# A new hand-kept instruction order, a recalibrated planner and a shorter last block in a fused attention and gated-MLP kernel

## The chip, the cores and the metric

The kernel runs on one core of a Trainium2 chip. The metric is the device time of one execution in microseconds, the median of several runs. Profiles come from one profiled execution, whose own time is given beside its span. TensorE is called PE here (its weight loads PEld), VectorE DVE, ScalarE ACT, GpSimd POOL, and the queue that issues the transfers SP.

## The reference

Two branches work on the same x (2048 rows of 512) and are mixed by a gate of one number per row:

```python
x = A_x                                    # (1, 2048, 512)
g = sigmoid((x * gate_w).sum(-1, keepdims=True))
# A: 32 query heads of 16, one shared key head and value head (wk, wv: 512 x 16)
q = heads(x @ wq); k = x @ wk; v = x @ wv
p = softmax(einsum("bhqd,bkd->bhqk", q, k) / 4)
a = heads_back(einsum("bhqk,bkd->bhqd", p, v)) @ wo
# B: a gated MLP with 1792 hidden columns
b = (sigmoid(x @ w_gate) * (x @ w_up)) @ w_down
return g * a + (1 - g) * b
```

All is fp32. A value may be split into a rounded part and a rest (`fp32r`), so that one product becomes three matrix multiplications.

## The kernel before

**The work.** Rows are cut into four blocks of 512 (`NB`). Attention goes in 32 units (`NU`), each a block of query rows with four heads. A unit has three kinds of PE work. First come 64 *maxima*: a matmul of 62 rows by 512 columns (line 1040), whose largest value per row DVE takes (line 1042). Then come 64 *scores*: a matmul of 64 rows by 512 columns (line 1049), of which ACT takes the exponential into a tile `p` (line 1051). Last come 16 *values* steps (line 931): each multiplies four `p` tiles with V, four 128x32 column tiles side by side, into bank 7. The MLP and the output projection are cut into 4404 *fill* matmuls of 64 rows by 512 columns (line 1019), which belong to jobs: `g` and `u` for gate and up, `d` for down, `a` and `e` for the output projection.

Maxima, scores and fills use half of the array's rows each, so they come in pairs: one matmul on the upper half, one on the lower, at the same time. Values use the whole array in four column tiles.

**The order.** Nothing is scheduled at run time. `ORDER` is a string, found by a search beforehand and kept in the file, of one character per step:

- a hex digit is a step of two halves: its two base-4 digits say what the upper and the lower half do (0 nothing, 1 a maximum, 2 a score, 3 a fill), so `f` is two fills and `6` a maximum beside a score;
- `V` is one values step, `T` turns the maxima of a finished unit (line 916), `G` is one group of the first projections (lines 798 and 855), and `.` is a pause of 25 units of the planner's clock that gives no instruction.

`plan()` walks through the string with a `State`, a model of the engines with a clock in units (one step of two halves is 100), and writes down the actions in the order in which they are then recorded for each engine. Each engine runs its own list in order; a last loop of `tile_kernel` ties them together so that no scheduler moves anything. So the constants at the top of the file do two things: they decided which orders the search held to be possible, and they set where the planner puts the work of DVE, ACT, POOL and SP between the steps.

**What the planner reckons with.** Steps share seven PSUM banks (0 to 6). `issue_m` takes the bank that has been free longest and marks it busy until `LATE` (from the step to the reader's start), plus the reader's cost on its engine's own clock (`RED` for a maximum), plus `TAIL` and `FREE`. `issue_s` does the same with `EXP`, `issue_f` and `settle` with the readers of a finished fill job, `issue_t` and `issue_g` likewise. A values step may come when all four of its exponentials are seen (`can_v`). `IN`, `OUT` and `FIRST` are what a change between paired steps and values costs on the planner's clock, `VALUES` a values step itself.

**The last block.** When the string is done, the last unit's sums (bank 7) are copied out in two halves on ACT, turned on PE, divided on DVE by their own sums, turned back, copied (three on ACT, one on DVE) and multiplied with the last rows of `wo` into banks 3 to 6. For two of the four output tiles PE first puts the sum so far into the bank (`so_far`, line 1077); ACT then copies those two out (line 1106) and DVE adds the other two (line 1108). Each tile is stored by its own transfer (line 1109).

Of the kernel before, what the change touches and what calls it, by code (L numbers as in the profile page):

```python
# [18 lines left out]
P = 128  # L19
# [20 lines left out]
LATE, FREE = 230, 50  # L40

RED, EXP, COPY, MIX, TAIL = 260, 212, 230, 275, 40


IN, OUT, FIRST, VALUES, TURN = 45, 45, 57, 371, 75
# [56 lines left out]
class State:  # L102
# [157 lines left out]
    def event(self, what, args):  # L260
# [15 lines left out]
        elif what == "send_max":  # L276
            self.max_ready[args[0]] = self.send(4, 16)
        elif what == "store":
            self.after(self.send(5, 136) + SAFE, "sums", *args)
        elif what == "sums":  # L280
            self.after(self.send(1, 8) + 2 * SAFE, "invert", *args)
        elif what == "invert":
            self.after(self.on("dve", self.now, 120), "send_inverse", *args)
        elif what == "send_inverse":
            self.after(self.send(1, 8) + SAFE, "spread", *args)
        elif what == "spread":
            u = args[0]
            at = self.send(1, 128)
            if u % 2 or u == NU - 2:
                self.task(2, at + 2 * SAFE, "divide", u)  # L290
        elif what == "out":
            at = self.send(1, 256)
            self.ba_release(args, at)
# [85 lines left out]
    def settle(self):  # L379
        for h in range(2):  # L380
            while self.at[h] is not None and self.at[h] == self.jobs[self.job[h]].n:
# [4 lines left out]
                if j.kind == "g":  # L386
                    self.acts.append(("gate", h, j, i))
                    at = self.on("act", at, COPY)
                elif j.kind == "u":
                    slot, free = self.take_h()  # L390
                    self.acts.append(("gated", h, j, i))
                    at = self.on("dve", max(at, free), MIX)
# [3 lines left out]
                self.free[i] = at + TAIL + FREE  # L396
# [8 lines left out]
    def gather(self, j, h, i, second, at):  # L405

        key = (j.b, j.i % NT)
        if key not in self.parts:
# [3 lines left out]
            return self.on("act", at, COPY)  # L412
        self.parts[key] += 1
        if not second and j.kind != "e":
# [3 lines left out]
            return self.on("act", max(at, free), COPY + 30)  # L418
        self.acts.append(("part", h, j, i, "sum"))
        at = self.on("dve", at, MIX)  # L420
# [38 lines left out]
    def issue_m(self, h):  # L459
# [4 lines left out]
        if self.mp[h] == min(self.mp) and self.mp[h] % (2 * NC) == 0:  # L464
            u = self.mp[h] // (2 * NC) - 1
            self.acts.append(("max_finish", u))
            self.maxima.append((u, self.on("dve", 0, 170)))

    def issue_s(self, h):
# [5 lines left out]
        at = self.on("act", self.now + LATE, EXP)  # L475
        self.free[i] = at + TAIL + FREE
# [3 lines left out]
        self.exps[e][1] = max(self.exps[e][1], at + TAIL + 80)  # L480
# [5 lines left out]
    def issue_v(self):  # L486
# [7 lines left out]
        if c == NC - 1 and u < NU - 1:  # L494
            self.acts.append(("finish", u))
            at = self.on("act", self.now + LATE, COPY) + TAIL
# [6 lines left out]
    def issue_t(self):  # L503
# [4 lines left out]
        at = self.on("dve", self.now + LATE, 260)  # L508
# [14 lines left out]
    def issue_g(self):  # L523
# [9 lines left out]
        else:  # L533
# [5 lines left out]
            if what == "keys":  # L539
                self.ba_take(("v", b), 1)  # L540
                at = self.on("dve", self.on("act", at, 250) + 50, MIX)
# [8 lines left out]
        self.free[i] = at + TAIL + FREE  # L550
# [24 lines left out]
    def step(self, code):  # L575
# [10 lines left out]
        elif code in "VG":  # L586
            if not self.full:
                self.now += IN
            if code == "V" and self.last != "V":
                self.now += FIRST  # L590
# [16 lines left out]
    "GGGGGGGG554G551G554GG551G541G554G55GG517G5d7ffG55fffd7ffGd7ffdf7ffdf7ffdff7cGd75ffG55fffd7ffGT5fffdf5ff7fG9ff7df"  # L607
    "fefffb7fff97fedfe7f9ff6fdbf7efdb7fedf6f35V969V696V9694V969V696V965Vb9ff7f9fe7ff9f6V97efdf6fedfb7f9ff7edef7f9VV69"
    "6V95eVTbff7dfe7f9ff7efdb7fedf6ff9ff6fdbf7bd.V696V9616V969Vb7efdf7fdbe7ffdbf6d.V696V969V55bVebf6ff9f7fedb7fedf9V6"
    "69VV69fbff6fd7bf9V6f9fff6deVT69V6f9f7fbdef7f9fe7fdbc6V969V696Vd56Vbbdeff6fdbbf6ff9f7d7VVd6bdff7fedbeff6fdbbV696V"  # L610
    "969V6bdeff6fbdbf7d7deVV6b9fff6fdbef6ff9f7bef9ff6.V55bVV9e6fffdb7ebfdefTfbf6ff97f9VVV697fff9fe7fedfaV696V969V6dbf"
    "7f9fe7ff9f6ffde7bVV9e7fefdf7bdfe7f9f7dVV6db7ffedbef7bf9f7eef5..V969V69eV696V97f9ff6ff9f7eff9ff6V9T6Vb96V9e7eff9f"
    "e7bf9fe7efd7VV969V6df6ff9ff6fdbf7bfde7VV9e7bff9f7eef9ff6fdbef6ff9f7d7VV96ffdff7bdebV696V969V69aV6dbf7f9fe7fedf6V"
    "V96bfff9f7edf6ff9fbef7dff6bVVT96V969.V6bdfef6fdbbf6ff9f7ebf9ff5VVV69feff6fbdef6fbdbVV69feff6fdb7f9ff6fbdf7ef9f7f"
    "d7edV5b7ffefd7V969V69a4V9652VV96fbff9f7edfe7f9ff6VV9fe7bf9feef7bedfb7fed7.VV9T6V96ffdf6fd7V9fbfef7bd7eV9f6fbfd7e"
    "dbV69ffefb7edbV696V969Vf5ebfef7bf9fe7ef9fe7VV969V6fdbf7edfb7fedf6fdb7VV9eb7ff9fe7ef9fe7bfde3V696V95b7V9a7VTeefdf"
    "f6bdbff6fdbd.VV6b7eff9f7ebf9ff7d7deVV6bedff6fbdbf6fbdef7df5V696VV9bf6ffdfb7ef9f7def6VV96bfff9fe7bf9fe7efdbf6V96d"
    "8VV697V96fdff6ff9f7dV6bdfef6fdbfb6ff9fef6fdbf75V97dV6T9V696V97efdf6fbdff6f9VV6bdbff6fdbef6ff9f7bef9ff6fV969V69aV"
    "7f9fe7efd7f9f7dVVV69feff6fbdbf6fbdef7bfedb7eVV965V96Vb9ef7fed7f9V69efff7db7eVT5bVe9fe7fbdef6fbdbff5faVV697fff9fe"
    "7fdef5ffbe7V969V696V979Vf6fedfb7ef9fe7df6f17VV96ffdf6fbdfb7f9V69efff6fdb7f9ff6fbdf7ef9fe.V69aV659V69VVTbef7ff9ef"  # L620
    "6ff9fb7ef9fe7df7df6VVV96bfff9f7edf6V96fbff9f7edf6ff9VV69bfff6ff9ef6ff9fb7ef9fe7dVV69ff7fdfb7ebff9f7edVV696V9eb7V"
    "9e7eff9f7ebfdef6fdbV696V9694V969V7VTedbfff6bedff6fbdbf6V97deff6ff9f7bfdef7bdV696V965VV96bfff9f7edf6ff9f7eVV96fbf"
    "fdfe7bf9fe7ef9fe7VV965Vbedbff6fdbef6ff9f7dbVV69ff7f9fe7ff9f6ffde7V969V696VT58Vebdef7bf9fe7ef9f7df278VV9e7eff9fe7"
    "bf9fe7efdb36V596VV9e7ffdb7edf7df6VV96ffbfdfb7ef9fe7bf9fe7fde7VV969Ve7bf9fe7ef9fe7bf9ff6fedff57d7VVV9fe7bf9fe7ef5"
    ".V9692VT689V6dbf7f9fe7ff9f6ffde7dVV6bbdff6fbf9fe7ef5ffaVV9692V5b79Ve6bffdef6fdbbf7ef9f7ebf9ff5V69f7ffdf7edeV6a9V"
    "696V596VV9b6fff9fe7bfd7edbVV6b9fff6fedbf7edfb7edf7dfTVVV69fbff6fd78c9Ve7fefdb6fbV9e7eff9fe7bV96feff9f7d7VV97efef"
    "9fe7bf9fe7efdb36Vd69fff7fbde7ff9V697V97fdeV69eV6bbdff6fbdef6fbdf7dbV696V969VV6Tbfffd7e9V6b9fff6fde7f9V696.V979V6"
    "edfbf5febf7efbd7d7VV9e6fff9f7ebf9ff6fdebf5.V696Vdfb7f9ff6dfe7f9VV6bedff7bdebf7ef9fe7bf9f7dVV69eV696V9e6fff9f7bef"
    "5VVTbedfff6bdbff6fd7df6VV9b6fff9f7dV6bedff6fbdbf6fbdef7bf9fe7df6fd7VVV96bfff5febeV96aVdb7efdbf7ef9f7ebf9ff6fdef7"
    "5VVV97efbf9f7edfe7.V969V6b9fff6fdebf6ff9f7deV696V96bV969VT56..Vbefdbf6fdbef6ff9f7d7VV96bfff9fe7ef9fe7bfde36V969V"  # L630
    "6d6dVV69ffbf7fbdbf6fbdef6VV96bfff9fe7bf9f7edVV6fbdef6fbdbf6fbdef7df6fbdVVV6bf9ff6fbdef6fd7dVV6Tbfffd7bbdf7fedbef"
    "f6fdbV696V969V696V96fdff6fbdf7bf9ff7edbf7f9V69f7V96dV6f5effbfd7e8eV969V69ff7f9fe7ff9f6ffde7V969V696VV9f6fdf6fbdf"
    "f6f9ff7bd2VVTb7efff9e7bff9f7edf6c.V9694VV9e6fff9f7ebf9ff6fde73aVV969V6bdeff6fdbbf6ff9f7ebf9ff5VV7ef9f7efde7fbde7"
    "V969VV697fff9fe7fdef6ffdb78VV9e6fff9f7ebf9ff6fde739V69V696VbT9V69ff7f9fe7ff9f6ffde..6VV969V6df6ff9ff6fdbf7bfde7V"
    "V9e6fff9f7bef9ff6fdbef6ff9f7d7VV96dfff7fbdebV696VV9e6fff9f7bef9ff6fd7dVV6bbdff6fbdef6fbdbf7ef5V969V696V9T6V969V6"
    "bfdef7bdebf7ef9f7ebf9ff5VVV69efff6fbdef6fbdbVV69feff6fdb7f9ff6fbdf7ef9f7fd7edV6bdfff7dbV6961V6b9V696VV9e6fff9fb7"
    "efdb7d7VV9e6fff9feb7f9fef7ef9f7deVV6T94V9fe7fdbf6fV96fbff9f7deV6deeffb7bdbV6fbdef6fbd7VV9fe7bf9fe7ef9fe7dV697ff."
    "V969V6db7ff9fe7fdef6ffdb78V969V696V969V69ff7f9fe7ff9f6ffde72VV9T7V9fef6f9fef6fbdbf6ff9VV6fbdef6fbdbf6fbdef7bf9f7"
    "d7VVV9e6fff9f7eef9ff6.V969V7edbf7efd7d7bVV97efef9fe7bf9fe7efdbf7ebdef7V969VV696V9f6fbf9f7efde7fbde7fd7f9VVVT6bff"
    "ff9ef6ff9fe7V969V6f97ff9V69efff6fdb7f9ff6fedf7bf9f7fed7dff6VVV9eb7ff9fe7ef9fe7bfdef6fd7dV69ff7ffdb7bfdf6VV9692V6"  # L640
    "9bfff6fdb7f9ffe7efdV696V96aV969V6a9V6T9V6dbf7f9fe7ff9f6ffd7d4VVV97efbf9fe7ef9fe7bfdeV696V96bVb597Vf9e7ffdfe7edff"
    "6f9V69bV6edfbf6fdbf7bfedb7efd7bf9VVV6ebdff6fbdef5fb7eVV9eb7ff9fe7ef9fe7dVVTbe7fff9e7bff9f7fede7fbd41V696V969V696"
    "V96bfff9f7edf6ff9VV6fbdef6fbdbf6fd7df7bVe9fe7fV969V6fbdef7d7d7VV9ef6ff9fb7ef9fef6ff9fb7ef9f7d7V96dV696VVTbfedff6"
    "fbdbf6fd7bf9V696V96eV95efffb7f9f7efdef7d7VV97bfdfefe7bdefb7dfeb24VV9e7bff9f7eef9ff6fdbe35V69.6....8V595V69VV69fe"
    "ff6fd7bV9a7fff9fe7eV96bfff9fe7ef9f7fedf6VVT96Vbbefdf7bef9ff6fdf6f9VV696Vb9ff7f9V697fffeed7fdbfaV6dbfeff6fbdbf6fb"
    "d7fed7dVV7b9ff7efde7befd7faV969V696Vbde7bfde7f9f7dVVV69efff6fd7bf9ff7edbfef7db7eVVT96Vb9ef7fedbf6fbdef6ff9f7d7f9"
    "VVV6bf9ff6fedbf6fbdV696V9a6V5fbdef7fbde7ff9fe7fdbf6fdfb7eV95f7fffed7V9a6V969V569VV6b9fff6fed7fbde7V96dV69fbff7f9"
    "f6ffde7bfdfe7beVV9T6V9f6fbf9f7deV69ffefb7edbV696Vb9e7ffedbf6V9e6fff9f7d7VV96fbffdfe7dfb7edff639VV6dbfbf6fbf9f6fe"
    "f9ffe4VV969V6bedff6fdbbf6fff97edVV69bV69efffbefbfefbfefbVVaTaVa.fefbfeVbeb2VVbfebffffeffbfefffbebeVVbebffefVaeVb"
    "bffebfefbfVea8Va..2Va8.2Va.8....2Va8..2Va8....2Va8..2.V.a8..2VaeceVaececc8Vaecc8c8V88.....VV"  # L650
# [11 lines left out]
def tile_kernel(ctx, tc, x_in, wq, wkv, wo, wg, wu, wd, consts_in, out):  # L662
# [405 lines left out]

# [4 lines left out]
    for i in range(2):  # L1073
# [88 lines left out]
```

## Time and profile before

| what | value |
|---|---|
| median of 3 runs | 1652.71 us (1652.61 to 1653.44) |
| profiled execution, its own time | 1652.89 us |
| its span in the trace | 1651.0 us |
| granted PE clock | 1.0 |
| busy share of the span: PE, PEld, DVE, ACT, POOL | 100%, 58%, 86%, 73%, 47% |
| mean DMA traffic | 60 GB/s |

1.9 us of the profiled execution's time lie outside the span. Busy time of PE is modelled from the instructions' sizes and overlaps, so 100% says only that PE always had something under way; the distance between the starts of its instructions is what can be read. The chain of work that ended last goes back from the last instruction through whatever released each one.

### The profile page before, as it was taken

The page shows a single profiled execution, that of the slowest core. Times are in us where ns is not written, and L with a number is a line of the kernel's source. Part 1 is how long each engine was busy: PE and PEld are TensorE (multiplying, and loading weights), DVE is VectorE, ACT ScalarE, POOL GpSimd, SP SyncE. Part 2 cuts the span into 40 slices and gives each one's busy share as a digit, 9 for nine tenths or more (in the row PEclk, how much of TensorE's full clock was granted, in tenths as well). Part 3 has the DMA queues.
Part 4 walks back from the last instruction along what each step waited for, and adds up shares of the span by engine and source line. Part 5 has one row for each costly group of instructions (what it writes and reads, how often), then busy time and mean ns, then how long its engine had stood idle before and what let it go on. Part 6 is the DMA issues. An engine that isn't in the chain of part 4 may idle for free.

```text
span 1651.0 us, 33584 instructions
## 1 busy us (share of the span) xinstructions
PE 1643.5 (100%) x12958; PEld 965.2 (58%) x12958; DVE 1424.5 (86%) x2419; ACT 1207.4 (73%) x2277; POOL 773.3 (47%) x598
## 2 busy tenths in 40 slices
PE   9999999999999999999999999999999999999998
PEld 7765556565555565656555656655566555555553
DVE  5799989899899998999988898989989989988941
ACT  4267777778767777687777777777777777777787
POOL 4524433548443336536455435444835432753341
PEclk9999999999999999999999999999999999999999
DMA  7412001115111112104111111211511101210001
GB/s 236 145 49 69 28 25 61 31 56 145 41 31 57 56 37 75 44 29 117 56 57 43 44 52 50 64 29 57 145 31 41 58 28 44 94 43 31 8 31 43
DMA packets 52085, 98.31 MB, mean 60 GB/s; under 512 B 17944, under 2 KB 19096, under 8 KB 50900
## 3 DMA queue, kind: packets, MB, share of 16 engines
q1 hardware_dynamic: 51924, 96.16, 19.0%
q8 instruction: 102, 1.67, 0.4%
q14 instruction: 59, 0.48, 0.1%
HBM read 74.25 MB, written 8.90 MB: 50 GB/s over the span
## 4 chain that ended last, share of the span: by engine, by line
PE 98%; ACT 1%; DMA 1%; SPq 0%; DVE 0%; issue 0%; ACTq 0%; DVEq 0%
PE bank L1019 31%; PE bank L931 30%; PE bank L1040 18%; PE bank L1049 17%; PE bank L798 2%; DMA consts<-consts 0%; PE bank L916 0%; SPq L895 0%; ACT x L717 0%; DVE qs L903 0%; DMA stage<-qd 0%; PE bank L1101 0%; SPq L702 0%; DVE ks L848 0%; ACT q L877 0%
## 5 line engine op out<-in xcount | busy, mean ns | idle before, releaser
L1042 DVE TENSOR_REDUCE mx<-bank 128x1 f32<-128x512 f32 x2048 | 1293.0, 684 | 141.6 <-PE bank L1040 71.9
L1051 ACT ACTIVATE p<-bank 128x512 f32<-128x512 f32 x2048 | 1086.4, 608 | 346.9 <-PE bank L1049 164.0
L1049 PE MATMUL bank<-qs,ks 64*128 64x512 f32 x2048 | 737.2, 412 | 0.0
L1040 PE MATMUL bank<-ks,qs 62*128 62x512 f32 x2048 | 732.0, 413 | 0.0
L931 PE MATMUL bank<-p,v_aug 128*32 128x512 f32 x4096 | 519.7, 601 | 0.0
L1049 PEld LDWEIGHTS bank<-qs,ks 64*128 64x128 f32 x2048 | 350.7, 185 | 186.4 <-DVE mx L1042 56.5
L1040 PEld LDWEIGHTS bank<-ks,qs 62*128 62x128 f32 x2048 | 345.9, 184 | 171.2 <-DVE mx L1042 61.7
L1019 PE MATMUL bank<-wd,hl 64*128 64x512 f32 x1344 | 257.0, 393 | 0.0
L931 PEld LDWEIGHTS bank<-p,v_aug 128*32 128x32 f32 x4096 | 95.2, 108 | 212.2 <-issue 205.0
L1019 PE MATMUL bank<-x,wg 64*128 64x512 f32 x672 | 204.1, 392 | 0.0
L1019 PE MATMUL bank<-xs,wg 64*128 64x512 f32 x672 | 203.7, 392 | 0.0
L1019 PE MATMUL bank<-xs,wu 64*128 64x512 f32 x672 | 201.7, 392 | 0.0
L1019 PE MATMUL bank<-x,wu 64*128 64x512 f32 x672 | 200.8, 392 | 0.0
L1019 PEld LDWEIGHTS bank<-wd,hl 64*128 64x128 f32 x1344 | 178.0, 185 | 25.6 <-DVE mx L1042 2.5
L903 POOL TENSOR_TENSOR qs<-stage,qs 16x1024 fp32r<-16x1024 f32 x62 | 148.7, 2398 | 4.8
L1003 POOL TENSOR_TENSOR ba<-ba,pa_d 128x512 f32<-128x512 f32 x48 | 61.7, 1288 | 135.4 <-DVE ba L982 106.9
L1019 PEld LDWEIGHTS bank<-x,wu 64*128 64x128 f32 x672 | 116.4, 186 | 13.6 <-issue 2.0
L1019 PEld LDWEIGHTS bank<-x,wg 64*128 64x128 f32 x672 | 116.9, 186 | 11.8 <-DVE mx L1042 1.7
L1019 PEld LDWEIGHTS bank<-xs,wg 64*128 64x128 f32 x672 | 116.8, 186 | 9.7 <-issue 0.2
L1019 PEld LDWEIGHTS bank<-xs,wu 64*128 64x128 f32 x672 | 115.8, 185 | 8.8
L692 POOL CAST hl<-h 128x512 fp32r<-128x512 f32 x56 | 34.3, 612 | 183.5 <-DVE h L1029 183.1
L901 POOL CAST qs<-stage 128x1024 fp32r<-128x1024 f32 x31 | 32.3, 1041 | 184.7 <-PE bank L1049 114.7
(86 smaller groups left out, 1065.8 us busy)
## 6 DMA issues: line engine op xcount, KB each, us to landing
rg<-wg SPq DMA_DIRECT2D x28, 512.0 KB
ru<-wu SPq DMA_DIRECT2D x28, 512.0 KB
rd<-wd SPq DMA_DIRECT2D x28, 512.0 KB
stage<-qd SPq DMA_DIRECT2D x192, 64.0 KB
xs<-x SPq DMA_DIRECT2D x16, 512.0 KB
xf<-x_in SPq DMA_DIRECT2D x16, 256.0 KB
qd<-q SPq DMA_DIRECT2D x16, 256.0 KB
ra<-wo SPq DMA_DIRECT2D x8, 512.0 KB
```

The source lines that it names most:

```text
L692: hi(hl[:, 0, :], raw)
L798: nc.tensor.matmul(ps, w[:, p, part(kc)], X[b, kc][:, q, :], start=i == 0, stop=i == 3 * KC - 1)
L901: (nc.scalar.copy if u == 0 else e.tensor_copy)(qs, stage)
L903: e.tensor_tensor(qs[r], stage[r], f32(qs[r]), op=ALU.subtract)
L931: nc.tensor.matmul(banks[7][32 * j:32 * j + 32, :], v_aug[:, c, :], PT.pop((u, c, j)), start=c == 0, stop=c == NC - 1)
L1003: nc.gpsimd.tensor_tensor(BA[b, t], BA[b, t], PA.pop((b, t)), op=ALU.add)
L1019: nc.tensor.matmul(banks[i], l, r, start=at == 0, stop=at == j.n - 1)
L1040: nc.tensor.matmul(banks[i], qs_t[u % 3][r, pr, part(qt)], ks[r, kb * 512:(kb + 1) * 512], start=True, stop=True)
L1042: nc.vector.tensor_reduce(MX[u][:, pr, h, qt, kb:kb + 1], banks[i], axis=AX.X, op=ALU.max)
L1049: nc.tensor.matmul(banks[i], ks[r, part(c)], qs_t[u % 3][r, pr, :], start=True, stop=True)
L1051: nc.scalar.activation(p, banks[i], AF.Exp, scale=0.25)
```

## The change

Three things change; the computation, the tiles and the number of instructions in front of the last block do not.

1. The constants of the planner. A reader on DVE and a reader on ACT get their own `LATE`, `TAIL` and `FREE`; nearly every reader gets its own cost; the pause before an exponential counts as seen falls from 40+80 units after its cost to 52+10; `FIRST` (57 units at the first values step of a run) goes and `OUT` grows from 45 to 94.
2. `ORDER` is another string. It has the same 512 `V`, 32 `T` and 24 `G`, the same 2048 maxima, 2048 scores and 4404 fills.
3. The last block: no `so_far`, one of the two copies out of bank 7 goes to DVE, two reciprocals of twice the width take the place of four, all four turned tiles are copied on ACT, and DVE adds all four outputs.

```diff
-LATE, FREE = 230, 50
-RED, EXP, COPY, MIX, TAIL = 260, 212, 230, 275, 40
-IN, OUT, FIRST, VALUES, TURN = 45, 45, 57, 371, 75
+LATE, LATE_A, FREE, FREE_A = 190, 200, 52, 65
+RED, GATED, SUM, ENDS, PARTS, INVERSE = 260, 258, 285, 60, 325, 70
+EXP, COPY, SCALED = 211, 210, 247
+TAIL, TAIL_A = 38, 52
+SEEN = 10
+IN, OUT, VALUES, TURN = 52, 94, 371, 50
...
 settle():                      # a finished fill job
-                    at = self.on("dve", max(at, free), MIX)
+                    at = self.on("dve", max(at, free), GATED)
+                    tail = TAIL + FREE
...
-                self.free[i] = at + TAIL + FREE
+                self.free[i] = at + tail       # TAIL_A + FREE_A for readers on ACT and for sums
...
 gather():
-            return self.on("act", at, COPY)
+            return self.on("act", at, SCALED)
...
-        at = self.on("dve", at, MIX)
+        at = self.on("dve", at, SUM)
...
 issue_m():
-            self.maxima.append((u, self.on("dve", 0, 170)))
+            self.maxima.append((u, self.on("dve", 0, ENDS)))
 issue_s():
-        at = self.on("act", self.now + LATE, EXP)
-        self.free[i] = at + TAIL + FREE
+        at = self.on("act", self.now + LATE_A, EXP) + TAIL_A
+        self.free[i] = at + FREE_A
...
-        self.exps[e][1] = max(self.exps[e][1], at + TAIL + 80)
+        self.exps[e][1] = max(self.exps[e][1], at + SEEN)
 issue_t():
-        at = self.on("dve", self.now + LATE, 260)
+        at = self.on("dve", self.now + LATE, PARTS) + TAIL
 step():
-            if code == "V" and self.last != "V":
-                self.now += FIRST
...
 ORDER = (                      # the ends of the two strings
-    ...VVbfebffffeffbfefffbebeVVbebffefVaeVbbffebfefbfVea8Va..2Va8.2Va.8....2Va8..2Va8....2Va8..2.V.a8..2VaeceVaececc8Vaecc8c8V88.....VV
+    ...VVebefbfefbfefbfefVbaVa.2Va8VefbefbfebV.Va..feffffbfefbffefffbfebVVebefbVefeeeVbbfbffbfebVVacececec8Vc8ccccV
...
     ou = [spare(f"ou_last{i}")[:, :2 * P] for i in range(2)]
-    for i in range(2):
-        nc.scalar.copy(ou[i], banks[7][:, i * 2 * P:(i + 1) * 2 * P])
-    def so_far(t):
-        nc.tensor.matmul(ps[t], ident, BA[NB - 1, t], start=True, stop=False)
-    so_far(0)
+    nc.scalar.copy(ou[0], banks[7][:, :2 * P])
+    nc.vector.tensor_copy(ou[1], banks[7][:, 2 * P:])
     for t in range(NT):
         nc.tensor.transpose(banks[t // 2][:, part(t % 2)], ou[t // 2][:, part(t % 2)], ident)
-    so_far(2)
...
-    for t in range(NT):
-        v = banks[t // 2][:, part(t % 2)].rearrange("p (j r) -> p j r", r=32)
-        rc = ap.tile(...)[:, :4]
-        nc.vector.reciprocal(rc, v[:, :, DH])
+    for i in range(2):
+        v = banks[i][:, :2 * P].rearrange("p (t j r) -> p t j r", t=2, r=32)
+        rc = ap.tile(...)[:, :8].rearrange("p (t j) -> p t j", t=2)
+        nc.vector.reciprocal(rc, v[:, :, :, DH])
...
-        (nc.vector.tensor_copy if t == NT - 1 else nc.scalar.copy)(o[t][r], oT[r, :P])
+        nc.scalar.copy(o[t][r], oT[r, :P])
...
-        nc.tensor.matmul(ps[t], o[t][r], WS["last"][r], start=t % 2 == 1, stop=True)
+        nc.tensor.matmul(ps[t], o[t][r], WS["last"][r], start=True, stop=True)
     for t in range(NT):
         ba = BA.pop((NB - 1, t))
-        if t % 2 == 0:
-            ba = spare(f"out{t}")
-            nc.scalar.copy(ba, ps[t])
-        else:
-            nc.vector.tensor_tensor(ba, ps[t], ba, op=ALU.add)
+        nc.vector.tensor_tensor(ba, ps[t], ba, op=ALU.add)
         nc.sync.dma_start(out[(n0 + t) * P:(n0 + t + 1) * P, :], ba)
```

More of the change, by code (lines that the diff above doesn't have):

```diff
@@ L282, in event @@
         elif what == "invert":
-            self.after(self.on("dve", self.now, 120), "send_inverse", *args)
+            self.after(self.on("dve", self.now, INVERSE), "send_inverse", *args)
         elif what == "send_inverse":
@@ L388, in settle @@
                     at = self.on("act", at, COPY)
+                    tail = TAIL_A + FREE_A
                 elif j.kind == "u":
@@ L395, in settle @@
                     at = self.gather(j, h, i, second, at)
-                self.free[i] = at + TAIL + FREE
+                    tail = TAIL_A + FREE_A
+                self.free[i] = at + tail
                 self.at[h] = self.bank[h] = None
@@ L417, in gather @@
             self.acts.append(("part", h, j, i, "apart"))
-            return self.on("act", max(at, free), COPY + 30)
+            return self.on("act", max(at, free), SCALED)
         self.acts.append(("part", h, j, i, "sum"))
-        at = self.on("dve", at, MIX)
+        at = self.on("dve", at, SUM)
         slot = self.halves.pop((j.key, "slot"), None)
@@ L495, in issue_v @@
             self.acts.append(("finish", u))
-            at = self.on("act", self.now + LATE, COPY) + TAIL
+            at = self.on("act", self.now + LATE, COPY) + TAIL_A
             self.v_free = at + FREE
@@ L540, in issue_g @@
                 self.ba_take(("v", b), 1)
-                at = self.on("dve", self.on("act", at, 250) + 50, MIX)
+                at = self.on("dve", self.on("act", at, 250) + 50, SUM)
                 self.ba_release((what, b, t), at)
@@ L549, in issue_g @@
         self.done += 300 if what == "turn" else 1200
-        self.free[i] = at + TAIL + FREE
+        self.free[i] = at + TAIL_A + FREE
         if self.first == len(GROUPS):
@@ L606 @@
 ORDER = (
[L607 to L650, printed above, removed]
+    "GGGGGGGG554G55G5141G554GG55G551G55G5G55G55GG55G55G5573G55Gdf7ffdf7ffdff7ffTfffdf7fffd7ffdf7ffdff6bdfbf7deb7fefd7"
@@ new lines @@
+    "bedf7f5VV9f7effbffedf6ff9ff6fdbf7bdfe7fbdf6ff9f7edc5V696V969V696V969V696V9694V969V6bdfef7dbe7fdfb7d7VVTebfdff7e9"
+    "fef7bdef7bde7VV979fff6f9ff7dV6f9fef6fdbf7edbf7efdb7edf7bdV6961..V69aV696V9694V969V696V969V6bdf7fedb7ff9fef7de39V"
+    "669V696V9TaV696Vdb6ffdf6fbdff6f9ff79VV69ff7f9febf7dfe7d7fd8VV69efff7bdefb7edfbe7bdV696V9689V5652VVbde7ff9f6ffdbf"
+    "6fdfb7edff6fbdf7bf9f7fed6..VV969V696VT96Vb97ffdfe6fdfb7f9ff6fedf7bd7VV96feff9f6fdf635VV9be7ff9fe7bf9fe7ef9ff6fd7"
+    "dVV79efbf7edbfe7bdeV6a9V696V969V696V969V5a6V9f7bfde7bfde7f9f7dVVTef6fffd6fbdf7bf9ff7fdfef7dbf6ffdb7edff6V96aV969"
@@ new lines @@
+    "V6949VV6bedff6fbdbf6fd7fdb7eVVdb6fbfde7bfde7befd7f9VVV69feff6f9fbf6f9fef6f1bV6958V696V969VV6Tfbff9ff7ed6fff9ff6d"
+    "fb7VV9fe6ff9fe7bf9fe7eV969VV6bdeff6f9fbf6f9fef6fdbf7bd7dVVV7e9fef7bdef7bdcff7ef9f7ebf9f7efde7f5VVV96bfff9f6fef9f"
+    "6fbf9V696V96aV969VV6de7ff9V6fTbff9ff7edef7bdef7f9fe7bfde7bdf7V969V6961V696VV9f6dffb79V69efff6f5fbfedbf7deV7b9fef"
+    "7ed7fbde7VV96dVb6f9ffe7bdVa5efff7db7eV969Ve6bfdf7bdfaV6bedffb7ed7VVTbfedff7bdef7bde7fd7VV9e6fff9f6fbf9f6fdf6f1bV"
+    "V6dfb7f9ff6ff9f7edf7dVV6f9fbf6f9fef6f9fbf6fdV6958.V69aV696V96V96bfff9f6fdf6f9VV6bdeff6f9fbf6f9fef6fdbf7d7d7VV9T6"
@@ new lines @@
+    "Vb9ef7fdebf6fdbf7de7bVV9ef6ff9fe7bf9fe7efd7f9VVV6f9fef6f9fbf6f9f7f9VV69feff7debf7dfe7beff9f5.V696V969V696V969Ve6"
+    "f9ffb7edbfe7bdefb7f9VVV6fedbfe7bf9fe7ef9f7dVVTef7bffd6ff9f7efdbf7edfb7f9ff6ff9f7d7VV95eeV696V9e6fff9f6fbf9f6fdf6"
+    "f17VV9694.V956Vbefbdfe7bf9fe7df6fdbVV6dbfef7bdebf7edfb7ebdVV696V9eb7ff9f7eef9f7fd7de7VVTb9V6edbff6f9fef6f9fbf6fd"
+    "7fd7d7VVV96fbff9f6fef9fa.V69aV696V9e6fffdb7bfde7befdbf6VVV95feff6fdbfb7fde7bfdV696.V965Vbebfdf7ebf9f7efd7d7eVVTb"
+    "efdff79ebff7debf7dVV6dbfef6f9fbf6f9fef6fdbf7d7d7VVV96fbff9f6fdf6f9V6bfd7febf9fe7fedbf6fbd7f9VV69feff7edbfe7bdeVV"
@@ new lines @@
+    "696V96bV9692V6968V5a9Ve7dbfef6fbd7f9f7dVVTebf7ffde6fbfdb7efd7db7VV97efff9f6fdf6fbdfe7f9V696V969V6dfb7f9ff6ff9f7e"
+    "fde7VV96fbffd7ebff9f6fdf6faVV96bfffde6fbfdb7efbed7Va96V965V96V965VV9e7bff9f7edf6fbdfe7fTff9VV6dfb7f9ff6fdef7beVa"
+    "96V969V6f9eff6f9f7f9f6VV9e7bff9f6fef9f6fbf9f7efde7d7V596.1VV696V96fdfV6bbdff6fd7bV9e7bff9f6fef9f6fbf9f7efd7edVVV"
+    "Tbef7ffdb6fbfde7bfde7dbVV6bedff6fbdbf6fbdef5V696V596VV9b7eff9f6fbf9f6fef9f7efd7db7VV9ef6ffdbf6fbdeVV696Vb9f6ffd7"
+    "dfaVb7bf9f7fef9ffef7ffd6VV95feff6fd8Ve5bfefb7ef5...bfedbfe7bdV6T9V696V969VV6b9fff6f9fef6f9f7febdVV6dfb7f9ff6ff9f"
@@ new lines @@
+    "7edf7dVV79fefe7bdefb7edbfe7bdVV6bdeff6f9f7f9f6VV96fbff9f6fdf6fbdfe7f9f7eff5V969V696V9T6Vb9f7efde7f9f7dVV6b9fff6f"
+    "9fef6f9fef6fdbf7db7eVVV97ebff9f7eef9f7dVV6bedff6fbdbf6fbdef6ff9f7d7V969.4V969V696V969V69feff6fdb7f9feef7df6VVV96"
+    "bfff9f6fdfb7ebff9faV6T1aV69feff6f9f7f9f6VVV9f6fbf9f6fef9f6fbf9f7efde7d7VVV9f6fbf9f6fef9f6fdf6V5b9f.V696V969V7edf"
+    "6ff9f7bfdef7bfd6VV96bfff9f6fdf6f9ff7dfaVV6f9fef6f9fbf6f9fef6f17VVVTbbfdff7e9fef7bdef7d7d7VV9e7bff9f6fef9f6fdf6.."
+    "VV9b7eff9f6fbf9f6fdf6fd4VV96fbffd7ebfd7f9feef36V9694V969V696V9a6V9e7fbf9f6fef9f6ffdb7d4VVV97eeff9fe7bf9fe7dfTfV6"
@@ new lines @@
+    "b9Ve6fbdfe7bf9f7d7VV9f6fef9f6fef9f6fbf9f7dfe7d7.VV96aV969V6edbff7ed7fd7bdVV6dbfef6f9fbf6f9fef5fbfe7bf9V696VV969V"
+    "69efffe79f7fd7edVV6Tbfff9f7fedbf7f9fe7df7d27VV96ffdfbe6V59bfffe7dbf7eV96aV9e7fbf9f5fefe7bfde7f9V69aV696V9616.V96"
+    "5VV9b7eff9f6fbf9f6fef9f4dVV6dfb7f9ff6ff9f7fedfa.V695VVTebf7ffde6fbfdb7efdb7deVV6b9fff6f9fef6f9ff79VV69feff6f9fbf"
+    "5f6VV9e6fff9f6fbf9f6fbf9f7efd7d7dVV6926.V969V696V96bfff9f6fdf6f9VV6b9fff6f9fef6f9fbf6fdbf7d7deVVVTbe7fffd6bbffd7"
+    "edfb7VV9f6fef9f6fbf9f6fef9f4dV696V969V696Vb9e7ffedb7efbde7dVV7bdef7bdef7bfde7bfde7bdfVVV6bedff6fd7bVb9f7efedb7eV"
@@ new lines @@
+    "95Ve7bdef7bd7eVb5efbfdeb7eVT.9aV69feff6f9f7fbde7fbdfecV695VV69bfff6f9f7f9f6ffd7VV9e6fff9f6fbf9f6fdf6f17VVd6bbffd"
+    "e7bfedb7febde7VV969V69efff6f9f7f9f6VV9e7bff9f6fef9f6fbf9f7efd7de7VVV97f9ff6ff9ff6fdef7bdfe7fdbfTff7efdff6bVVV9e7"
+    "bff9f6fef9f6VV9e6fff9f6fbf9f6fbf9f7efd7d7dVVV6bedff7bf9fe7ef9f7d7VV96efff9f6fbf9f6fef9ff6.V96aV969V69a4V9652V965"
+    "VVbdfTeff6ffdb7fbdf6ff9ff6fdbf7edfb7fed714V969V6a9V696V969V696V969V6bdeff7bdef7bdef7d7faVV9e7bff9f6fef9f6fdf6f17"
+    "VVV97bfef9f6fbf9f6fef9f4eVV979fff6f9ff7ef9ff7ed2VV6T9Vb7ef9fe7bf9fe7ef9f7df7de7VV96dfV6b9fff6f9fef6faV596VVdb6fb"
@@ new lines @@
+    "fdb7efdb7edf7dVV69bfff6f9f7f9f6V9f6fef9f7fff9f6fef9f7efdb7deV696V969V696V9T6V97ff9ff6fdbf7efdb7V96edV69aVV6f9fbf"
+    "5fefb7ef9f7efd6V96dVb6bfdfb7ef9fe7df6fdbVV6b9fff7edbf7edbef7dVVV6dfb7f9ff6ff9f7efdbfeaVV69aV696V5bdbff7debV6Tbff"
+    "f9f7fedef7bdef7bdfe7d7fd7dVVV69fbff6f5fbf9fef7edf6.V969V696Vbdb7efbde7bfedb7efbdc6VV9692.V659VV6bdbff6f9fef6f9fb"
+    "f6fd4VV97fedf6ff9ff6fdb7fbdVV6bedffb7ef9fe7bf9fe7fed7fTfdbVVV6bf9ff6fedbf6Vb96V96feff9f6fdf7d6VV9bf6ff9f7ebf9f7e"
+    "fde7befd7f9VV6961.V659Vbef7bfd7d7eV96fffdb7ebfd7fedbeff6f9f7f9feV696V969VV6T9Vb6fdbf7edbef7df6VV9b7eff9f6fbf9f7e"
@@ L651 @@
+    "ef9f7efdb4dV696V596VV9e7bff9f6fef9f6fbVVde6fbfdb7efdb7ebfdef6fd7bVVV9ef7fdb7d7Vebefdfbf6f9Va7f9ff7de7eV96aV969.V"
+    "69efffbebfffefbeVVTbfafffefbeb.VVefbfefbfefbebfeVVbebVefbfebVebfebffefbfVVebefbfefbfefbfefVbaVa.2Va8VefbefbfebV."
+    "Va..feffffbfefbffefffbfebVVebefbVefeeeVbbfbffbfebVVacececec8Vc8ccccV"
 )
@@ L1072, in tile_kernel @@
     ou = [spare(f"ou_last{i}")[:, :2 * P] for i in range(2)]
-    for i in range(2):
-        nc.scalar.copy(ou[i], banks[7][:, i * 2 * P:(i + 1) * 2 * P])
-    def so_far(t):
-        nc.tensor.matmul(ps[t], ident, BA[NB - 1, t], start=True, stop=False)
-    so_far(0)
+    nc.scalar.copy(ou[0], banks[7][:, :2 * P])
+    nc.vector.tensor_copy(ou[1], banks[7][:, 2 * P:])
     for t in range(NT):
         nc.tensor.transpose(banks[t // 2][:, part(t % 2)], ou[t // 2][:, part(t % 2)], ident)
-    so_far(2)
     on = [spare(f"on{i}")[:, :P] for i in range(2)]
     o = []
-    for t in range(NT):
-        v = banks[t // 2][:, part(t % 2)].rearrange("p (j r) -> p j r", r=32)
-        rc = ap.tile([P, DH], F32, tag="rc", name=f"rc_last{t}", bufs=2)[:, :4]
-        nc.vector.reciprocal(rc, v[:, :, DH])
-        nc.vector.scalar_tensor_tensor(on[t // 2].rearrange("p (t j e) -> p t j e", t=2, e=DH)[:, t % 2],
-                                       v[:, :, 0:DH], gsig[:, n0 + t:n0 + t + 1],
-                                       rc.unsqueeze(2).to_broadcast([P, 4, DH]), op0=ALU.mult, op1=ALU.mult)
+    for i in range(2):
+        v = banks[i][:, :2 * P].rearrange("p (t j r) -> p t j r", t=2, r=32)
+        rc = ap.tile([P, DH], F32, tag="rc", name=f"rc_last{i}", bufs=2)[:, :8].rearrange("p (t j) -> p t j", t=2)
+        nc.vector.reciprocal(rc, v[:, :, :, DH])
+        for k in range(2):
+            t = n0 + 2 * i + k
+            nc.vector.scalar_tensor_tensor(on[i].rearrange("p (t j e) -> p t j e", t=2, e=DH)[:, k],
+                                           v[:, k, :, 0:DH], gsig[:, t:t + 1],
+                                           rc[:, k].unsqueeze(2).to_broadcast([P, 4, DH]), op0=ALU.mult, op1=ALU.mult)
     for t in range(NT):
```

## The prediction, written before the changed kernel ran

> **What bounds the kernel now.** I read the page first: who is busy, and whose work the last chain runs through.
>
> ```profile
> PE 1643.5 (100%) x12958; PEld 965.2 (58%) x12958; DVE 1424.5 (86%) x2419; ACT 1207.4 (73%) x2277; POOL 773.3 (47%) x598
> ...
> PE 98%; ACT 1%; DMA 1%; SPq 0%; DVE 0%; issue 0%; ACTq 0%; DVEq 0%
> ```
>
> Busy PE proves nothing, but the chain does: 98% of it is PE following PE, DVE and ACT together about 1%. Next the stretches and the groups by line, for the readers of the banks (columns: DVE is the third engine, ACT the fourth).
>
> ```profile
> 100.00:1500.00 1400.00, 1400.00 (x11323) 815.37 (x11319) 1265.91 (x2141) 1050.31 (x1982) 668.82 (x509) 1.00 0.18 55
> ...
> 1610.00:1641.00 31.00, 31.00 (x211) 11.42 (x208) 3.92 (x6) 29.07 (x59) 7.54 (x7) 1.00 0.10 22
> ```
>
> ```profile
> L1042 DVE TENSOR_REDUCE mx<-bank 128x1 f32<-128x512 f32 x2048 | 1293.0, 684 | 141.6 <-PE bank L1040 71.9 <-PE bank L1049 44.1 <-PE bank L916 2.9
> ...
> L1040 PE MATMUL bank<-ks,qs 62*128 62x512 f32 x2048 | 732.0, 413 | 0.0
> ```
>
> In the main stage DVE is busy 1265.91 of 1400 us (0.90) and idles before a maximum because PE has not delivered: PE leads, DVE follows. From 1610 us ACT is busy 29.07 of 31 us: there it may lead. So what counts is how many things PE does in a row and what each costs. The chain in a quiet stretch shows it (start, length, what):
>
> ```profile
> 861.39 0.99 PE bank L931 x8
> ...
> 869.81 2.71 PE bank L931 x24
> ...
> 875.29 0.99 PE bank L931 x8
> ...
> 877.18 1.00 PE bank L931 x8
> ```
>
> L931 is the values step, eight matmuls each. In the order string 31 steps of paired halves lie between the first row and the second, 11 between the second and the third, 3 between the third and the fourth. So with p for a paired step, v for a values step and r for the two changes of array shape around a run of values: 31p+v+r = 8.42, 11p+3v+r = 5.48, 3p+v+r = 1.89 us. The first less the third gives p = 0.233; the second then gives v = 0.86, and r = 0.33. **Every separate run of values costs 0.33 us**, whatever its length.
>
> A check on the last stage, from the last maximum to the last values step:
>
> ```profile
> L1042 DVE TENSOR_REDUCE mx<-bank x2048: 626/682/695, 27.1 to 1587.6; 128x1 f32<-128x512 f32 x187
> ```
>
> ```profile
> 1621.32 1.31 PE bank L931 x8
> ...
> 1623.30 1.29 PE bank L931 x8
> ...
> 1625.26 1.29 PE bank L931 x8
> ...
> 1627.22 1.29 PE bank L931 x8
> ...
> 1629.18 1.29 PE bank L931 x8
> ...
> 1634.39 1.00 PE bank L931 x8
> ```
>
> ```profile
> PEld bank L931 <- ACT p L1051: 5.8, 17, 0.9
> ```
>
> Behind the last maximum the string has 107 paired steps, 24 values in 20 runs: 107x0.233 + 24x0.86 + 20x0.33 = 52.2 us. Its matmul starts some 0.41 us (row L1040) before the reduce at 1587.6, so at 1587.2, and the last values end at 1640.9 (below): 53.7. The 1.5 us between are in the rows: five values steps of 1.29 to 1.31 instead of 0.99, 0.30 each, waiting for exponentials (last row, wait of PEld on ACT). The accounting closes.
>
> **The change, part by part.**
>
> *The order string.* I count in both strings, merging a half step on one side with the next on the other.
> - Runs of values: 379 before, 350 after, with 512 values in both. 29 x 0.33 = **-9.6 us**, wholly on PE's chain.
> - Paired steps 4279, then 4282: 3 x 0.233 = **+0.7**.
> - Turns of the maxima (`T`) that stand between paired steps instead of beside values: 14 to 18. Each costs from nothing to one change of shape (0.33), so 0 to 1.3; I take the middle, **+0.6**.
> - End stage: the string held back 84 fills, 192 behind the last maximum instead of 108, with the same 91 scores. Where ACT set the pace, PE now has fills to do. Pauses written into the string there fall from 26 to 5, in front of it they go from 25 to 27. I let the five waits of 0.30 go but for one: **-1.3** (0 to -1.5).
>
> *The planner's constants* cost nothing themselves; they allow a bank to be used again sooner. Before, a maximum's bank was reserved for 230+260+40+50 = 580 units, after for 190+260+38+52 = 540; at 2.33 ns a unit (100 units = p) 1.35 and 1.26 us. Both are over five steps (1.17) and under six (1.40), so the least spacing stays six. What the readers need of it is 0.41 (matmul) + 0.68 (reduce) = 1.09, which leaves 0.30 for signals and DVE's queue. But it is used up more often: with p, v and r laid along each string, the maxima's banks that are taken again after just six steps go from 326 to 553, the exponentials' from 558 to 621, 290 more together. Bounds: nothing (no wait), or all of the 40 units (0.093 us) given up at each of 227 more maxima, 21 us. Below nothing: existing waits could go too, -1. The near row is the chain: 0.30 spare is over three times what is given up, and DVE's share of it reads 0%. I take 7 ns for each of 290, **+2**. A values step may now come 473 units after its last score instead of 562, 0.21 us earlier; I cost that at 0 to 1 us within the 2, since the values rows outside the end stage read 0.99 to 1.00.
>
> DVE, POOL and the transfers do the same work in front of the last block. Since 10 us go and the last stage grows by 8.5 us (148x0.233 + 24x0.86 + 17x0.33 = 60.7 against 52.2), the main stage must shrink by about 15 us of 1490, which lifts DVE's share there from 0.90 to 0.91. That is the cover on which the sum rests.
>
> *The last block.* Rows of the timeline (in brackets the engine's idle time before and what ended it):
>
> ```profile
> 1638.78 2.13 PE L931 MATMUL bank<-p,v_aug 128*32 128x512 f32 x16
> ...
> 1640.84 1.12 PE L1077 MATMUL bank<-ba,consts 128*128 128x512 f32 x2
> ...
> 1641.80 0.60 PE L1081 MATMUL bank<-consts,ou_last 128*128 128x128 f32 x4
> ...
> 1642.28 0.18 DVE L1089 RECIPROCAL rc_last<-bank 128x4 f32<-128x4 f32 x1 [4.46 <-PE bank L1081]
> ...
> 1642.70 0.17 DVE L1089 RECIPROCAL rc_last<-bank 128x4 f32<-128x4 f32 x1
> ...
> 1644.32 1.99 PE L1101 MATMUL bank<-re,o_last 64*128 64x512 f32 x8
> ...
> 1645.52 0.69 DVE L1108 TENSOR_TENSOR ba<-bank,ba 128x512 f32<-128x512 f32 x1 [0.80 <-PE bank L1101]
> ...
> 1646.38 0.69 DVE L1108 TENSOR_TENSOR ba<-bank,ba 128x512 f32<-128x512 f32 x1 [0.17 <-PE bank L1101]
> ...
> 1647.49 0.40 SPq L1109 DMA_DIRECT2D out<-ba  x1
> ```
>
> The turns (L1081) stand behind `so_far` (L1077); without it they can start about when ACT's first copy is there, some 0.2 to 0.4 sooner. Two reciprocals fewer in DVE's chain: 2 x 0.17 = 0.34. So the last matmuls start about 0.6 earlier, and the first output at 1644.9 instead of 1645.5. Then four adds on DVE follow each other: 4 x 0.69 = 2.8, to 1647.7; before, the last ended at 1647.07. SP's last transfer, issued at 1647.49 before, moves by **+0.2** (from -0.6, if the adds keep up with the matmuls, to +1.2, if the chain is not shortened).
>
> *Sum*: -9.6 + 0.7 + 0.6 - 1.3 + 2 + 0.2 = -7.4 us on the profiled 1652.89, whose span is 1651.0: 1645.5, span 1643.6. The median is 0.18 lower than the profiled run: 1645.3, say **1645**. With every lower bound it is 1640.7, with 6 us of waits 1649.3.
>
> **The rivals.**
>
> *VectorE sets the main stage* (the slower end). If DVE's 0.90 is in truth its limit, since it cannot run ahead of PE by more than the seven banks, the last maximum stays at 1587.6 and the longer last stage comes on top: +8.5, less 1.3 at the end, plus 0.2: 1660. It decides when DVE cannot do its 2048 maxima 15 us sooner. Against it: 141.6 us in which DVE was idle right before a maximum, with PE as the releaser. The Trainium skill, Perfetto Trace Analysis, section Identifying the Most-Contended Engine, tells one to rank PE by the share of weight loads and not by matmuls; by it DVE with 86% stands above PE with 58%, and work saved on PE would then bring nothing: 1660, this rival. The trace does not agree: in its chain DVE has 0%, and PE's time between the weight loads is the changes of shape, which no other engine fills. Chance 0.06.
>
> *Bank waits eat the gain* (no change). The 553 maxima at six steps wait on average 13 to 25 ns, or the values wait in half their runs for 50 ns: +7 to +14 where I put 2; the sum comes out between -2.4 and +4.6, 1650 to 1657, around 1652. For it: margins are now means and readers vary (626 to 695 ns in the row above). Against it: 0.30 us spare in six steps. Chance 0.11, of which 0.08 lies within 0.2%.
>
> *The order does not carry through*: runs on PE do not start when the string says, because a weight split on POOL or a transfer comes late near the end, where the held-back fills wait for the last projection weights. POOL is busy 7.54 of 31 us there; one late split is 1 to 2 us: 1646 to 1647, within my range and its chance.
>
> **How the numbers follow.** A measurement of this kernel can tell about 0.2%, 3.3 us. My forecast of 1645 has 0.83: -7.4, from -12 (every lower bound) to -3.4 (6 us of waits), which are all faster by over 0.2%. Faster 0.83; within 0.2% 0.09 (0.08 of the waits, 0.01 of a half-decided DVE); slower 0.08 (0.03 of the waits, 0.05 of DVE). The range goes from 1640.5 (waits of the old order gone too) to 1649.5 and leaves out the slower rivals.
>
> **What would show it.** Right: values runs in the chain still 0.99 + 0.86 for each further one, 29 fewer; the last maximum near 1572; no run of values of 1.29 in the last 20 us but one or two; the last block from the last values to the end at 10.1 us, give or take 0.6; DVE's share in the main stage near 0.91. Wrong: the last maximum still near 1587 (DVE leads); or p in the chain over 0.236 where maxima are dense, with PEld waiting for DVE between paired steps (bank waits); or values of over 1.1 in the main stage (exponentials seen too early).

## The result and the profile after

The changed kernel takes 1645.93 us in the median (1645.38 to 1647.36, six runs) against 1652.70, a ratio of 0.9959 with a 95% interval of [0.9946, 0.9972]: 0.4% faster. The forecast was 1645, range 1640.5 to 1649.5. The span of the profiled execution fell from 1651.0 to 1643.8 us; 1643.6 had been worked out.

The page after gives the span and the busy time of each engine:

```profile
span 1643.8 us, 33572 instructions
...
PE 1636.6 (100%) x12954; PEld 982.3 (60%) x12954; DVE 1418.7 (86%) x2419; ACT 1202.2 (73%) x2275; POOL 773.0 (47%) x598
```

The main stage in the windows (DVE third, ACT fourth), the maxima by line, and the waits of the weight loads for them (total, times, longest):

```profile
100.00:1500.00 1400.00, 1400.00 (x11344) 833.50 (x11342) 1264.89 (x2152) 1052.47 (x1994) 670.46 (x512) 1.00 0.19 55
```

```profile
L1048 DVE TENSOR_REDUCE mx<-bank x2048: 624/681/694, 26.8 to 1574.1; 128x1 f32<-128x512 f32 x187
```

```profile
PEld bank L1055 <- DVE mx L1048: 81.4, 111, 0.8
PEld bank L1046 <- DVE mx L1048: 65.2, 124, 0.8
```

Lines are six further down than before (1040 is now 1046, 1049 is 1055, 931 is 937). The last maximum starts at 1574.1 instead of 1587.6 us. The last two rows need care. The first weight load behind a values run comes 0.84 us after the last one of the run in any case, and the view puts that down to whatever released the load last. Before, the same two rows read as follows:

```profile
PEld bank L1040 <- DVE mx L1042: 61.7, 77, 0.8
PEld bank L1049 <- DVE mx L1042: 56.5, 68, 0.8
```

That is 145 waits of 0.82 us on average, nearly all of them values runs. After, it is 235 waits of 0.62, so many of them must be short. This is one:

```profile
1408.81 0.18 PEld L1055 LDWEIGHTS bank<-qs,ks 64*128 64x128 f32 x1 [0.18 <-DVE mx L1048]
```

Taken one by one, the waits of the two rows that do not stand right behind a values run go from 6 (1.7 us together) to 79 (15.7 us, 0.20 each). Those are waits for a bank that DVE still reads; the lighter kernel below shows it, where none of them is left.

The chain in the last stage, where the old order had five values steps of 1.29 to 1.31 us (start, length, what):

```profile
1601.94 1.00 PE bank L937 x8
...
1603.60 1.00 PE bank L937 x8
...
1605.26 0.99 PE bank L937 x8
...
1606.92 0.99 PE bank L937 x8
...
1610.19 1.93 PE bank L937 x16
...
1617.39 1.85 PE bank L937 x16
...
1626.43 1.89 PE bank L937 x16
```

None waits 0.3 us any more: single steps read 0.99 to 1.00 (the very last 1.04, since the chain has it to its own end), and double ones 1.85 (0.99 + 0.86), two of them 0.04 and 0.08 above that.

The last block in the timeline:

```profile
1633.11 1.07 PE L937 MATMUL bank<-p,v_aug 128*32 128x512 f32 x8
1634.25 0.37 ACT L1078 COPY ou_last<-bank 128x256 f32<-128x256 f32 x1 [1.36 <-PE bank L937]
1634.65 0.42 DVE L1079 COPY ou_last<-bank 128x256 f32<-128x256 f32 x1 [0.61 <-ACT ou_last L1078]
...
1635.14 0.21 DVE L1088 RECIPROCAL rc_last<-bank 128x8 f32<-128x8 f32 x1
...
1636.80 1.99 PE L1102 MATMUL bank<-re,o_last 64*128 64x512 f32 x8
...
1637.96 2.48 DVE L1105 TENSOR_TENSOR ba<-bank,ba 128x512 f32<-128x512 f32 x4 [1.47 <-PE bank L1102]
1638.68 2.12 SPq L1106 DMA_DIRECT2D out<-ba  x4
```

From the end of the last values (1634.18) to the end of the span it takes 9.6 us; before it was 1651.0 - 1640.9 = 10.1. So of the span's 7.2 us, 6.7 were won in front of the last values' end and 0.5 behind it.

### The profile page after: what moved, and what is told of

It reads as the page before. It is cut to its first block, busy times and chain, and to the rows that moved or that the text cites. A ratio compares the mean times of both kernels' runs of the same rounds, so it can differ in the third digit from the quotient of the medians.

```text
span 1643.8 us, 33572 instructions
## 1 busy us (share of the span) xinstructions
PE 1636.6 (100%) x12954; PEld 982.3 (60%) x12954; DVE 1418.7 (86%) x2419; ACT 1202.2 (73%) x2275; POOL 773.0 (47%) x598
## 4 chain that ended last, share of the span: by engine, by line
PE 99%; DVE 0%; ACT 0%; issue 0%; DVEq 0%; POOL 0%; POOLq 0%
PE bank L1025 31%; PE bank L937 30%; PE bank L1046 18%; PE bank L1055 17%; PE bank L804 4%; PE bank L822 0%; PE bank L922 0%; DVE ba L1105 0%; PE bank L861 0%; PE bank L1102 0%; ACT x L723 0%; DVE on L1091 0%; DVEq L1155 0%; POOL v_aug L816 0%; PE bank L1097 0%
## 5 line engine op out<-in xcount | busy, mean ns | idle before, releaser
L937 PE MATMUL bank<-p,v_aug 128*32 128x512 f32 x4096 | 512.1, 601 | 0.0
L1025 PE MATMUL bank<-xs,wu 64*128 64x512 f32 x672 | 205.0, 393 | 0.0
```

Of the source, the lines that this page charges most:

```text
L937: nc.tensor.matmul(banks[7][32 * j:32 * j + 32, :], v_aug[:, c, :], PT.pop((u, c, j)), start=c == 0, stop=c == NC - 1)
L1025: nc.tensor.matmul(banks[i], l, r, start=at == 0, stop=at == j.n - 1)
```

## The experiments

Theory A: PE's own row of work sets the time. The new string has 29 runs of values fewer at a third of a microsecond each, and pays some of it back in waits for banks that DVE has not yet read. Rivals: the gain comes from the held-back fills and the last block; or DVE leads. The constants and the string go together in every exchange, since neither string is allowed under the other's constants; what the constants alone do to the order of work on DVE, ACT, POOL and SP is not shown.

**Cutting 29 runs in two.** In 29 places spread over the new string, two values steps that stand together were parted:

```diff
-  V V x        # x a paired step
+  V x V
```

> The new kernel with 29 of its double runs of values cut in two (V V x becomes V x V, x a paired step), so 379 runs as in the old string; nothing else moves, and the values steps only come later. Theory A (each separate run costs PE 0.33 us): 29 x 0.33 = 9.6 us more, 1655.5, or some 2 us less if a pause between values gives the readers time that bank waits took before: 1653 to 1656. Theory B (the gain comes from the held-back fills and the last block, and runs are hidden): unchanged, 1646.

Measured: 1655.48 us (1655.17 to 1656.92), beside a kernel before of 1652.87; ratio 1.0018 [1.0009, 1.0026]. That is 9.6 us more than the new kernel and the whole gain gone. In its timeline the last values stand here:

```profile
1643.04 1.06 PE L937 MATMUL bank<-p,v_aug 128*32 128x512 f32 x8
```

They end at 1644.10 instead of 1634.18, 9.92 us later, which is 0.34 us a run. Of the relief of bank waits that I allowed for, little came: the short waits fall from 79 to 71. With the rest of the string untouched, the runs alone move the kernel from faster than the old one to slightly slower.

**The last block by itself, both ways.** The two blocks were exchanged whole.

```diff
# old order, new end: the constants and ORDER of before, everything behind plan()'s loop of after
# new order, old end: the constants and ORDER of after, everything behind plan()'s loop of before
```

> The old constants and string with the new last block. From the last values step to the end the traces have 10.09 us before and 9.62 after. Theory A (the new block's chain is shorter by itself): 0.5 us less, 1652.2. Rival (four adds on VectorE cost more, and the 0.5 us comes from what stands in front of the block): up to 1.2 us more, 1653.9.

Measured: 1652.12 us against 1652.87, ratio 0.9996 [0.9987, 1.0005].

> The new constants and string with the old last block. Theory A (order and block add up): 1645.9 + 0.5 = 1646.4. Rival (the old block suits the new order as well or better): 1644.7 to 1645.9.

Measured: 1646.99 us (1646.18 to 1647.32), ratio 0.9964 [0.9951, 0.9977], so 1.1 above the new kernel (0.9 when each is taken against the kernel before that ran beside it). The first alone cannot be told from no change. The four traces agree with each other: from the end of the last values to the end of the span it takes 10.1 and 10.3 us with the old block, 9.6 and 9.4 with the new. So the new block is worth 0.5 to 1.1 us, and within that order and block add up.

**VectorE made lighter.** Each maximum over half its columns, in both kernels:

```diff
-        nc.vector.tensor_reduce(..., banks[i], axis=AX.X, op=ALU.max)
+        nc.vector.tensor_reduce(..., banks[i][:, :256], axis=AX.X, op=ALU.max)
```

> The new kernel, each maximum taken over 256 of its 512 columns: VectorE does a good deal less per maximum (what is left out is the other half of the columns in the maximum that is subtracted before the exponential). Theory A (PE's chain leads, VectorE costs it only bank waits): the waits go, 13.3 us of time over the bare rows in the new trace of which some 5 belong to single half steps, so 4 to 9 us less, 1637 to 1642, and no more. Rival (VectorE leads the main stage): 20 us less or more, 1626 or under.

> The old kernel, each maximum over 256 of its 512 columns (the other half of the columns is left out of the maximum). It measures the old order without VectorE's waits, beside the new one without them (1639.9). Theory A (the new order wins 9.6 us of PE's own work and gives some 3 us back in bank waits that VectorE makes): the old loses less, 2 to 4 us, 1649 to 1651, so that the distance between the two grows from 6.9 to 9 to 11 us. Rival (the waits are the same in both orders): also 6 us less, 1646.9, distance 6.9.

Measured: the new one 1639.86 us (1639.49 to 1639.98), ratio 0.9922 [0.9908, 0.9935]; the old one 1651.22 (1650.53 to 1651.52), ratio 0.9989 [0.998, 0.9998]. In the windows of the lighter new kernel DVE is busy 845 of 1400 us instead of 1265:

```profile
100.00:1500.00 1400.00, 1400.00 (x11389) 823.76 (x11387) 845.28 (x2159) 1056.60 (x2003) 676.13 (x515) 1.00 0.18 55
```

```profile
L1048 DVE TENSOR_REDUCE mx<-bank x2048: 360/424/429, 27.3 to 1568.2; 128x1 f32<-128x256 f32 x187
```

```profile
PEld bank L1055 <- DVE mx L1048: 52.8, 63, 0.8
PEld bank L1046 <- DVE mx L1048: 36.9, 44, 0.8
```

The waits for maxima are now 107 of 0.84 us, nothing but values runs: the short ones are gone. A third of DVE's work taken away brings 6.1 us, 0.4%, so DVE does not lead. The old kernel becomes only 1.8 us faster (against 1653.01 beside it). Without DVE's waits the two kernels lie 11.4 us apart (11.2 when each is taken against the kernel before that ran beside it), with them 6.8: **the new kernel wins some 11 us, the last block's part included, and gives 4 to 5 back** to waits that DVE makes.

**VectorE made heavier.** One small copy behind every second maximum (`scr` holds two numbers per row and is set to zero at the start):

```diff
+        if h == 0:
+            nc.vector.tensor_copy(scr[:, 0:1], scr[:, 1:2])
```

> The old kernel with one more small VectorE copy (128 x 1, from SBUF to SBUF) behind every second maximum, 1024 in all; the shortest copies in the traces, 128 x 4, follow each other at about 0.1 us, so some 60 to 100 us of VectorE work on top of 1425. Theory A (PE leads; VectorE has room): bank waits grow, 3 to 25 us more, 1656 to 1678. Rival (VectorE leads): all of it, 60 to 100 us more.

> The new kernel with the same 1024 small copies. Theory A (its banks are taken again at six steps more often, 553 against 326 times, and its main stage is 15 us shorter): it suffers more than the old one by some 3 to 10 us, so the distance shrinks from 6.9 to between 4 and -3. Rival (the tighter spacing costs nothing): the distance stays 6.9.

Measured: the old order 1661.7 us (1661.37 to 1661.82), ratio 1.0052 [1.0035, 1.0069]; the new one 1658.54 (1658.16 to 1658.98), ratio 1.0032 [1.0019, 1.0045]. DVE's busy time rose by some 50 us in both; here is the heavier new kernel's page:

```profile
PE 1649.0 (100%) x12954; PEld 993.8 (60%) x12954; DVE 1471.9 (89%) x3444; ACT 1204.1 (73%) x2275; POOL 772.6 (47%) x598
```

The old kernel became 8.7 us slower, the new one 12.6. Both take most of DVE's extra work in their stride, the new one less so: the distance falls to 3.2 us. Taken with the lighter kernels, the advantage of the new one is 11.4, 6.8 and 3.2 us as DVE's load goes up.

**Searching on.** The findings point to fewer runs and pauses at a spacing that DVE can follow, so I let a plain local search of mine go on from the new string, with the same planner:

```diff
- aim: the planner's clock at the end
+ aim: the same, plus (28 - d) / 4 for each bank taken again d < 28 units after its planned release
```

> The new kernel with its string searched on from where it stands, with the same planner and one thing added to the aim: a bank that is taken again within 28 units of its planned release costs a quarter of what is missing to 28. 348 runs of values instead of 350, 4283 paired steps instead of 4282, 13 written pauses instead of 32. Theory A (runs and pauses are PE's own work, tight reuse makes bank waits): 2 x 0.33 + 19 x 0.06 - 0.23 = 1.6 us less, and about 1 us of waits less: 1643.3. Rival (the planner's last units are below what readers vary by): no change, 1645.9.

> The new kernel once more, beside the searched one on the same chip: 1645.9 by either theory.

Measured on the same chip: 1644.33 us (1643.17 to 1644.78), ratio to before 0.9946 [0.9934, 0.9959]; the new kernel again 1646.1 (1645.21 to 1646.67), 0.9958 [0.9945, 0.9972]. The five runs of the one all lie under the five of the other, by 1.8 us in the median, so it beats both kernels, if by little. The weight loads' waits for maxima, by rows:

```profile
PEld bank L1046 <- DVE mx L1048: 76.7, 128, 0.8
PEld bank L1055 <- DVE mx L1048: 72.0, 93, 0.8
```

That is 221 waits of 0.67 us, and a higher mean means fewer short ones among them: 58 (12.0 us) instead of 76 (15.0 us) in the new kernel beside it. By the lighter kernel 79 short waits cost 6.1 us, 0.08 each, so 18 fewer are worth some 1.4 us, an estimate; two runs of values less one paired step more are 2 x 0.33 - 0.23 = 0.4. Together that is the 1.8 us measured. So the record speaks for the added aim having done what it was meant to, though the two shares are not tested apart. The expected 19 x 0.06 us for the written pauses is not needed for it; a pause gives no instruction, and no run here shows that it costs PE time by itself.

## Why the prediction was right, point by point

- *What bounds the kernel.* Right, and now shown: 29 runs put back cost 9.6 us, a third less DVE work saves 6.1. By the share of weight loads, one of the two measures for TensorE that the Trainium skill names in Perfetto Trace Analysis, section Identifying the Most-Contended Engine (the other, FLOPs over the peak, was not worked out), DVE (86%) stands before PE (58%) and this change would bring nothing. The measurement decides otherwise here. One reading in the argument against that rival was loose: the time in which no weights are loaded is mostly the values steps themselves (512 x 0.86 = 440 us), and the changes of shape are 379 x 0.33 = 125 us.
- *Runs of values, -9.6.* Right: 0.34 us a run instead of 0.33, so -9.9.
- *Bank waits, +2.* The term that was mis-sized. The half-width pair puts it at 4 to 5 us. I took 7 ns for each of 290 tight reuses and had no row for it; about 15 ns is what they cost. The error was to argue from the old order, from its 0% of DVE in the chain and from a mean of 0.30 us to spare: the old planner had kept 40 units more in hand at every tight reuse. In the planner's own books, banks behind a maximum that are taken within 5 units of their planned release go from some 70 to some 275. It stayed well inside the bounds of 0 and 21 us. Of the sign that I named for it, half appeared: PEld does wait for DVE between paired steps, but the paired step, fitted over the stretches between values runs from 100 to 1500 us, went from 0.233 to 0.235 us and not over 0.236.
- *The end stage, -1.3.* The five late values steps are gone, 1.5 us; two double runs are 0.04 and 0.08 us long. Right. By the accounting the stage from the last maximum's matmul (1574.1 - 0.41) to the last values' end (1634.18) was to take 60.7 us; it took 60.5. The last maximum was put near 1572 and stands at 1574.1; in the lighter new kernel it stands at 1568.2, so the waits account for its being late.
- *Steps (+0.7) and turns (+0.6).* Not tested one by one. Up to the last values' end I had -7.6 in all and the trace has -6.7; the larger waits alone would make it -5.6 to -4.6. Runs and end stage are better by 0.5 together, and what the rest is, some 1 us among the untested terms, stays open. So that the whole sum came out within a microsecond is in part luck: the waits were put too low by about as much as the other terms together were put too high.
- *The last block, +0.2.* Better than put: -0.5 in the trace, -0.8 and -1.1 in the exchanges. The last matmuls start 2.62 us behind the last values instead of 3.41 (0.8 sooner; I had 0.6), and four adds take 2.48 us and not 2.8, because they follow each other at 0.62.
- *DVE's share of the main stage*, 0.91 forecast: it stayed at 0.90 (1264.89 of 1400). Instructions in that window went from 2141 to 2152, half a per cent, where I had expected one; busy time counts overlapping ends once, so it follows the load less than I assumed.
- *The rivals.* DVE as the leader is ruled out by the half-width and by the heavier kernels. Bank waits did take part of the gain, but 4 to 5 us and not the 7 to 14 that would have made it no change. Nothing came late from POOL in the last stage: the one wait of a fill's weight load on POOL there is as long as a values run.

```profile
PEld bank L1025 <- POOL wa L699: 0.8, 1, 0.8
```

## What to carry to other kernels

Where one engine is never idle, count what it does in a row, and look for what it pays between two kinds of work: here three equations from four rows of the chain gave the price of a change, and a count in the program gave the gain. A planner that gives up margin wins the work that it packs closer and pays in short waits; price those waits by the new spacing, not by what the old one cost. To tell the two apart, make the follower lighter in both versions: the distance without waits is the gain in work, and the difference to the real distance is what was given back.

## What the runs showed that I had not expected

- The copies out of the two halves of bank 7, one on ACT and one on DVE, do not run side by side: DVE's starts at 1634.65, 0.03 us after ACT's ended, with ACT as its releaser. The two take 0.82 us together where two on ACT took 0.65 before, so giving one of them to DVE won nothing there.
- 1024 extra copies of 128x1 read 144 ns each, 147 us in all, but raised DVE's busy time by only some 50 us and the old kernel by 8.7: rows of DVE overlap. In the heavier new kernel such a copy starts at 900.33, 0.08 us before the maximum in front of it ends.
- The sum of DVE's waits is in no row by itself. A row of waits whose mean lies under the 0.84 us of a values run (0.62 after, 0.67 in the searched string) was the sign of them.
